# One level of Strassen's scheme for the products with w_in and w_k, and a second part ordered by a list scheduler

## The chip, the cores and the metric

One core of a Trainium2 chip runs the whole program. The metric is the device time of one execution in microseconds (us). TensorE (PE) multiplies, ScalarE (ACT) and VectorE (DVE) do the element-wise work, GpSimd (POOL) a few small copies, and SyncE (SP) issues the DMAs.

## The reference

x has shape (4, 3072, 256), so 12288 tokens of 256 channels. Cut to what matters:

```
X = rfft(x, axis=1);  Y = softshrink(complex_linear(X; w_r, w_i, b_r, b_i), 0.01);  y = irfft(Y)
h = y @ w_in                       # 256 -> 2048
g = h * tanh(softplus(h))          # "Mish"
x2 = g @ w_out                     # 2048 -> 256
xk = mu_k * x2 + (1 - mu_k) * x2_prev        # x2_prev: the token before, 0 at the start of a sequence
xr = mu_r * x2 + (1 - mu_r) * x2_prev
k = relu(xk @ w_k);  v = (k * k) @ w_v       # 256 -> 1024 -> 256
out = sigmoid(xr @ w_r2) * v
```

## The kernel before

Every product of real data is made of three TensorE products, because each operand is split into a rounded high part and a low rest: high by high, high by low, low by high. The weights come in as 64-bit words and are decoded on ACT and DVE, one piece of 256 columns (or rows) at a time, by `decode` and the `Weights` pipeline.

Part 1 is the Fourier part. It runs over 48 units, 4 sequences by 12 groups of frequencies: `emit_F`, `emit_M`, `emit_I` on TensorE, the evacuations `post_F`, `post_M`, `post_M2`, `post_I` between them, and the butterflies (`f1_ops`, `f3_ops`) as background work on DVE. In the units of the last sequence ACT and DVE also decode w_in and w_out (`win_piece`, `wout_piece`) and a rest of the other weights (`park_piece`), two steps a unit. The final butterflies of sequences 1 to 3 (six `f3_ops` jobs) run in part 2.

Part 2 takes 24 blocks of 512 tokens. For each of the 16 slices of 128 columns of w_in a step does: `emit_H` (6 matmuls of 512 columns into a PSUM bank), Mish on ACT, `dve_g` (a cast to the high part and a subtraction for the low), and `emit_acc` three steps later (6 matmuls with w_out into two accumulators). A block's accumulators are copied out (`evac`), mixed with the token before (`token_mix`) and split, all in SBUF. Between the steps of the next block stand 8 `emit_K` (6 matmuls of 512 columns each), 8 `emit_V` (12 of 256 columns each) and 2 `emit_R` (12 of 256 columns each, then a sigmoid). Where each stands is written out by hand in `PLAN`. All weights of part 2 lie in SBUF. Four PSUM banks (`psw`) rotate for the products, so a product that waits for its evacuation doesn't hold up the next. Each engine runs its instructions in the order in which they are written.

All matmuls go through the helper on line 155, all activations through line 152, tensor_tensor through 146 and scalar_tensor_tensor through 149.

Of the kernel before, what the change touches and what calls it, by code (L numbers as in the profile page):

```python
# [39 lines left out]
NPARK = 5  # L40
PARK_AT = (6, 15)

F3_PART1 = {(1, 4): [(0, 0)], (1, 8): [(0, 1)]}
F3_PART2 = {1: (1, 0), 3: (1, 1), 5: (2, 0), 8: (2, 1), 10: (3, 0), 14: (3, 1)}


SPLIT_AT = (13, 14)
EVAC_AT = 3
K_BUFS = 4
G_BUFS = 3  # L50
FILL = (900, 1500, 0)


PLAN = {
    'first': dict(K=[22, 23, 25, 27, 29, 31, 34, 36], V=[27, 27, 30, 30, 33, 33, 39, 39],
                  R=[35, 35], mix=[19, 20, 24, 25], end=40),
    'mid': dict(K=[23, 24, 25, 26, 29, 31, 35, 36], V=[28, 28, 30, 30, 34, 34, 39, 39],
                R=[33, 33], mix=[19, 20, 23, 25], end=40),
    'late': dict(K=[23, 24, 26, 28, 30, 32, 33, 36], V=[26, 28, 29, 31, 33, 35, 37, 39],
                 R=[28, 29], mix=[19, 20, 23, 25], end=40),  # L60
    'last': dict(K=[22, 23, 24, 25, 27, 28, 29, 29], V=[26, 27, 28, 29, 30, 31, 32, 33],
                 R=[25, 25], mix=[19, 20, 21, 23], end=35),
}
# [3 lines left out]
            23, 24, 25, 26, 30, 31, 28, 32, 29, 33, 34, 35, 41, 42, 36, 43, 37, 38, 44, 45, 39, 40, 46, 47]  # L67
LINES_G = [4, 5, 6, 7, 12, 13, 14, 15]
# [8 lines left out]
def dft_constants():  # L77
# [32 lines left out]
    return lay(fwd), lay(inv), sel  # L110


@with_exitstack
def tile_fft_mix_moe_channel_mix(
# [44 lines left out]
    w_dr = [dram.tile([128, 2, 512], F32, name=f"w_dr{i}") for i in range(9)]  # L159
    y_dr = [dram.tile([2, 128, 24, 128], F32, name=f"y_dr{b}") for b in range(NB)]  # L160

# [4 lines left out]
    y_p = pool(ctx, "y", 1)  # L166
    yhl_p = pool(ctx, "yhl", 2)

    mu = cst.tile([128, 2, 2], F32, name="mu")
    mu1 = cst.tile([128, 2, 2], F32, name="mu1")  # L170
# [243 lines left out]
    wt = {}  # L414

    def load_mix(h):
        raw = pools["st"].tile([128, 2, 256], F32, tag="raw", name="wraw", bufs=2)
# [18 lines left out]
    raws = []  # L436

    def raw_piece(src):
        p, tag = raws[1][raws[0] % len(raws[1])]
        raws[0] += 1  # L440
        raw = p.tile([128, 512, 2], I32, tag=tag, name="raw", bufs=2)
# [4 lines left out]
    def decode(raw, parts, scale=1.0):  # L446
        hw, lw = raw[:, :, 1], raw[:, :, 0]
        tl = {}

        def a0():  # L450
            sg = tl["sg"] = pools["st"].tile([128, 512], F32, tag="sg", name="sg")
            return [lambda: act(sg.bitcast(I32), hw.bitcast(F32), ACTF.Copy, scale=14000.0),
                    lambda: act(sg, sg.bitcast(I32), ACTF.Sign)]

        def v0():
            q = tl["q"] = pools["st"].tile([128, 512], F32, tag="q", name="q", bufs=3)
# [11 lines left out]
        def a2():  # L468
            tl["p"] = parts(tl["q"])
            return [lambda hi=hi, v=v: act(hi, v, ACTF.Copy, scale=scale) for hi, lo, v in tl["p"]]  # L470

        def v2():
            if scale == 1.0:
                return [lambda hi=hi, lo=lo, v=v: tt(lo, v, hi.bitcast(F32), SUB) for hi, lo, v in tl["p"]]
            return [lambda hi=hi, lo=lo, v=v: stt(lo, v, scale, hi.bitcast(F32), MULT, SUB)
                    for hi, lo, v in tl["p"]]
# [3 lines left out]
    def win_piece(i):  # L480
        raw = raw_piece(w_in[:, 256 * i:256 * i + 256])
        cs = slice(256 * i, 256 * i + 256)
        w = wt["in"]
        return decode(raw, lambda q: [(w[:, 0, :, cs], w[:, 1, :, cs],
                                q.rearrange("p (k f) -> p k f", k=2))])

    def wout_piece(i):
        raw = raw_piece(w_out[256 * i:256 * i + 256, :])

        def parts(q):  # L490
            ts = [mat.tile([128, 2, 256], F32R, tag="m", name="wo") for _ in range(2)]
            wt["out", 2 * i], wt["out", 2 * i + 1] = ts
            return [(ts[k][:, 0, :], ts[k][:, 1, :], q[:, 256 * k:256 * k + 256]) for k in range(2)]
        return decode(raw, parts)


    parked = ([w_k[:, 256 * i:256 * i + 256] for i in range(4)]
              + [w_v[256 * i:256 * i + 256, :] for i in range(4)] + [w_g])

    def park_piece(i):  # L500
        raw = raw_piece(parked[i])
        tl = {}

        def parts(q):
            t = tl["t"] = yhl_p.tile([128, 2, 512], F32R, tag="yl", name="wp")
            return [(t[:, 0, :], t[:, 1, :], q)]
        a0, v0, v1, a2, v2, a1 = decode(raw, parts)
        return a0, v0, v1, a2, lambda: v2() + [lambda: nc.sync.dma_start(out=w_dr[i], in_=tl["t"].bitcast(F32))], a1

    def fetch():  # L510
        for i in range(4):
            nc.sync.dma_start(out=wt["v"][:, :, 2 * i:2 * i + 2, :].bitcast(F32),
                              in_=w_dr[4 + i].rearrange("p s (c f) -> p s c f", c=2))
        nc.sync.dma_start(out=wt["g"].bitcast(F32), in_=w_dr[8].rearrange("p s (c f) -> p s c f", c=2))
        for c in range(8):
            wt["k", c] = mat.tile([128, 2, 2, 128], F32R, tag="m", name="wkt")
            src = w_dr[c // 2].rearrange("p s (h k f) -> p s h k f", h=2, k=2)
            for z in range(2):
                nc.sync.dma_start(out=wt["k", c][:, z].bitcast(F32), in_=src[:, z, :, c % 2, :])
# [27 lines left out]
    NBLK = NB * N // 512  # L547
    yt = {}

    def load_y(j):  # L550
        b, o = divmod(j, N // 512)
        t = y_p.tile([128, 2, 512], F32, tag="y", name="y")
        for h in range(2):
            nc.sync.dma_start(out=t[:, h, :], in_=y_dr[b][h, :, 4 * o:4 * o + 4, :].rearrange("p n f -> p (n f)"))
        yt[j] = t

    yhl = {}

    def split_y(j, h):
        if h == 0:  # L560
            yhl[j] = (yhl_p.tile([128, 2, 512], F32R, tag="yh", name="yh"),
                      yhl_p.tile([128, 2, 512], F32R, tag="yl", name="yl"))
        hi, lo = yhl[j][0][:, h, :], yhl[j][1][:, h, :]
        y = yt[j][:, h, :]
        l = [lambda: tt(lo, y, hi.bitcast(F32), SUB)]
        if j:
            return [lambda: act(hi, y, ACTF.Copy)], l
        return [], [lambda: V.tensor_copy(hi, y)] + l


    def part1():
        with ExitStack() as es:
# [6 lines left out]
            raws[:] = [0, [(st_p, "raw"), (st_p, "raw"), (yhl_p, "yh")]]  # L579
# [152 lines left out]
            NU = NB * NT  # L732

            pe, bg.clock = START
            x_at, y_at = bg.clock, 0.0
            for u in range(NU):
# [9 lines left out]
                if u == NU - NT - 1:  # L746
                    wt["in"] = big.tile([128, 2, 2, 2048], F32R, tag="big", name="win")
                    todo = [lambda: win_piece(0)]
# [5 lines left out]
                    wq = Weights(todo[:6] + late + todo[6:])  # L754
                    wq.load(3)
# [3 lines left out]
                elif PARK_AT[0] <= u < PARK_AT[1]:  # L759
                    dec = 1  # L760
                    if u == PARK_AT[0]:
                        wq = Weights([lambda i=i: park_piece(i) for i in range(NPARK)])
# [35 lines left out]
                if b == NB - 1 and t == 10:  # L798
                    bg.drain()
                    load_y(0)  # L800
# [3 lines left out]
            for h in range(2):  # L804
                emit(split_y(0, h)[1])
# [7 lines left out]
    def part2():  # L813
        with ExitStack() as es:
            ch_p = pool(es, "ch", 2)
            gh_p = pool(es, "gh", G_BUFS)
            x2_p = pool(es, "x2", 1)
            xk_p = pool(es, "xk", 1)

            pool(es, "gap", 1).tile([128, 16], F32, name="gap")  # L820
            xr_p = pool(es, "xr", 1)
            kk_p = pool(es, "kk", 2)
            sg_p = pool(es, "sg", 1)
            psw = pool(es, "psw", 4, space=PSUM)
            psa = pool(es, "psa", 1, space=PSUM)
            psv = pool(es, "psv", 1, space=PSUM)

            b1 = big.tile([128, 8192], F32R, tag="big", name="b1")
            wt["v"] = b1[:, 0:4096].rearrange("p (s c f) -> p s c f", s=2, c=8)
            wt["g"] = b1[:, 4096:5120].rearrange("p (s c f) -> p s c f", s=2, c=2)  # L830
            xk = [b1[:, 1024 * i:1024 * i + 1024].rearrange("p (c f) -> p c f", c=2) for i in (5, 6, 7)]
            xk = [tuple(xk[:2]), (xk[2], xk_p.tile([128, 2, 512], F32R, name="xkl1"))]
# [234 lines left out]
```

## Time and profile before

| | |
|---|---|
| median of 3 runs | 1982.35 us (1982.24 to 1982.41) |
| span of the profiled execution | 1979.9 us; its time around the span isn't listed by itself, and the median of the runs lies 2.45 us above it |
| TensorE busy, matmuls | 1958.0 us (99%), 10084 |
| DVE busy, ACT busy | 1141.4 us (58%), 929.0 us (47%) |
| part 1, part 2 on TensorE | to 327.2 us, then to 1975.2 us |
| granted TensorE clock | 1.00 in each stretch that was read |

A matmul's busy time overlaps that of the next one, so that the time from start to start, and not the duration, tells what a matmul takes. For ACT and DVE the durations of instructions that follow each other overlap by about 0.1 us.

### The profile page before, as it was taken

To read this page: it belongs to the slowest core of one execution; us is meant where nothing else is said; L and a number is where in the kernel's file an instruction comes from. 1 tells how busy PE (TensorE), PEld (TensorE's weight loads), DVE (VectorE), ACT (ScalarE), POOL (GpSimd) and SP (SyncE) were. 2 spreads that over 40 slices of the span, in tenths; PEclk is the share of its full clock that TensorE was granted. 3 is DMA by queue.
4 is the path that set the end of the run, shared out by engine and by line. 5 is a ranking of instruction groups with operands and counts; after the bars stand their busy time and mean duration, and the time that the engine had idled before them with its cause. 6 is when DMAs were issued, how large, how long until landed. Compare 5 with 4: busy or idle time off the path is not lost.

```text
span 1979.9 us, 25685 instructions
## 1 busy us (share of the span) xinstructions
PE 1958.0 (99%) x10084; PEld 1686.2 (85%) x10084; DVE 1141.4 (58%) x2183; ACT 929.0 (47%) x1525; POOL 13.2 (1%) x28
## 2 busy tenths in 40 slices
PE   6999999999999999999999999999999999999999
PEld 5888888888888888888888888888888888888888
DVE  8999976665654754465375445555544544444444
ACT  2422286344544554454445444444544544454455
POOL 0000000000000000000000000000000000000000
PEclk9999999999999999999999999999999999999999
DMA  9445276111011010101101001011000000000000
GB/s 279 150 138 170 70 245 200 39 32 65 22 33 54 22 44 11 54 22 33 54 22 54 1 22 54 5 33 38 22 1 22 22 11 12 22 23 1 22 11 22
DMA packets 104554, 106.66 MB, mean 54 GB/s; under 512 B 7017, under 2 KB 85489, under 8 KB 103409
## 3 DMA queue, kind: packets, MB, share of 16 engines
q1 hardware_dynamic: 104432, 105.02, 16.7%
q8 instruction: 79, 1.29, 0.3%
q14 instruction: 43, 0.34, 0.1%
HBM read 62.53 MB, written 42.47 MB: 53 GB/s over the span
## 4 chain that ended last, share of the span: by engine, by line
PE 97%; DMA 1%; DVE 1%; ACT 0%; issue 0%; SPq 0%; DVEq 0%; ACTq 0%
PE a L155 26%; PE hps L155 26%; PE v L155 14%; PE kps L155 13%; PE yps L155 7%; PE bps L155 4%; PE xps L155 4%; PE zps L155 3%; DMA a<-in_x_dram 1%; DMA w_dr<-wp 0%; DVE g L146 0%; ACT sg L152 0%; SPq L266 0%; DVE q L149 0%; ACT q L152 0%
## 5 line engine op out<-in xcount | busy, mean ns | idle before, releaser
L863 DVE CAST gh<-u 128x512 fp32r<-128x512 f32 x384 | 163.2, 425 | 747.5 <-PE a L155 598.2
L155 PE MATMUL a<-gh,wo 128*128 128x512 f32 x1536 | 536.3, 390 | 0.0
L155 PE MATMUL hps<-yh,win 128*128 128x512 f32 x1536 | 534.7, 389 | 0.0
L152 ACT ACTIVATE u<-hps 128x512 f32<-128x512 f32 x384 | 229.7, 598 | 525.0 <-PE hps L155 368.8
L155 PEld LDWEIGHTS hps<-yh,win 128*128 128x128 f32 x1536 | 288.3, 188 | 60.3
L155 PEld LDWEIGHTS a<-gh,wo 128*128 128x128 f32 x1536 | 288.4, 188 | 58.0
L155 PE MATMUL a<-gl,wo 128*128 128x512 f32 x768 | 299.9, 390 | 0.0
L155 PE MATMUL hps<-yl,win 128*128 128x512 f32 x768 | 298.8, 389 | 0.0
L155 PE MATMUL kps<-b,wkt 128*128 128x512 f32 x960 | 280.1, 390 | 0.0
L155 PE MATMUL v<-b,kh 128*128 128x256 f32 x1536 | 275.8, 281 | 0.0
L146 DVE TENSOR_TENSOR gl<-u,gh 128x512 fp32r<-128x512 f32 x384 | 263.6, 687 | 3.6
L155 PEld LDWEIGHTS v<-b,kh 128*128 128x128 f32 x1536 | 243.7, 190 | 7.6
L155 PE MATMUL v<-b,kl 128*128 128x256 f32 x768 | 215.8, 281 | 0.0
L155 PEld LDWEIGHTS kps<-b,wkt 128*128 128x128 f32 x960 | 179.1, 188 | 36.1
L152 ACT ACTIVATE ka<-kps 128x512 f32<-128x512 f32 x192 | 115.0, 599 | 185.5 <-PE kps L155 185.5
L155 PEld LDWEIGHTS hps<-yl,win 128*128 128x128 f32 x768 | 144.1, 188 | 29.9
L155 PEld LDWEIGHTS a<-gl,wo 128*128 128x128 f32 x768 | 144.5, 188 | 26.6
L146 DVE TENSOR_TENSOR kl<-ka,kh 128x512 fp32r<-128x512 f32 x192 | 132.5, 690 | 32.8 <-ACT ka L152 19.1
L155 PEld LDWEIGHTS v<-b,kl 128*128 128x128 f32 x768 | 144.1, 188 | 0.0
L152 ACT ACTIVATE ka<-ka 128x512 f32<-128x512 f32 x192 | 121.4, 632 | 6.3
L152 ACT ACTIVATE kh<-ka 128x512 fp32r<-128x512 f32 x192 | 121.4, 632 | 6.3
L146 DVE TENSOR_TENSOR g<-g 128x128 f32<-128x128 f32 (+3 forms) x272 | 107.5, 433 | 1.2
(80 smaller groups left out, 1926.8 us busy)
## 6 DMA issues: line engine op xcount, KB each, us to landing
b_dr<-bs SPq DMA_DIRECT2D x48, 256.0 KB, 2.2
g<-b_dr SPq DMA_DIRECT2D x8, 1536.0 KB, 6.8
y<-y_dr SPq DMA_DIRECT2D x48, 256.0 KB, 3.2
out_dram<-r SPq DMA_DIRECT2D x48, 256.0 KB, 2.2
y_dr<-g SPq DMA_DIRECT2D x80, 64.0 KB, 1.6
w_dr<-wp SPq DMA_DIRECT2D x9, 512.0 KB, 5.9
a<-in_x_dram SPq DMA_DIRECT2D x8, 512.0 KB, 6.2
y_dr<-g SPq DMA_DIRECT2D x32, 128.0 KB, 1.9
```

The source lines that it names most:

```text
L146: V.tensor_tensor(out=o, in0=a, in1=b, op=op)
L152: S.activation(out=o, in_=i, func=f, **kw)
L155: T.matmul(out=o, lhsT=l, rhs=r, start=start, stop=stop, **kw)
L863: return [lambda: V.tensor_copy(hi, u), lambda: tt(lo, u, hi.bitcast(F32), SUB)]
```

## The change

**The scheme.** The products with w_in and w_k are made in blocks of 2 by 2 by 2: the 256 channels in two halves, 1024 tokens in two halves of 512, and 256 columns of the weight as two slices of 128. Of the 8 block products the Winograd form of Strassen's scheme needs 7 (each of three matmuls). Its sums of weights are made once, at decoding (`pair_pieces`), and stored in DRAM (`h_dr`, `k_dr`); its sums of data are made once per 1024 tokens (`mix_sum`, `part_hi`, `part_lo`, in `moving`). Its sums of results are made in PSUM: ACT copies a partial result from one bank to another, later matmuls add to the copy, and DVE adds two results to SBUF (`k12`, `k22`).

**Two phases.** Phase A does all 12 superblocks of 1024 tokens through w_in and w_out, 8 groups each. The mixed tokens go to DRAM (`xk_dr`, `xr_dr`). Phase B reads them back and does w_k, w_v and the gate, 4 groups for each superblock. In phase A the sums of w_in come from DRAM group by group, four DMAs each, into a ring of two groups (`load_ring`). w_v and the gate's weight are decoded late in phase A.

**The order.** The class `Plan` takes each step with an engine, an assumed duration, a due time and the steps it needs, runs through the time of the five engines and calls the steps in the order that comes out. The hand-written `PLAN` and `FILL` go. TensorE's banks are now x, z, c, d, one buffer each, and four accumulators.

The diff, cut to its core:

```diff
+    def pair_pieces(w, dst, i, m, field, stage):          # part 1; two raw pieces, 512 KB each
+            def sums():
+                return v1() + [lambda: tt(s(1), s(4), s(0), SUB), lambda: tt(s(2), s(6), s(1), SUB),
+                               lambda: tt(s(5), s(6), s(4), SUB), lambda: tt(s(7), s(3), s(2), SUB)]
+            def highs():
+                t = f["t"] = stage()
+                return [lambda: act(t[:, 0:4, 0, :], f["s"][:, 0:4, :], ACTF.Copy),
+                        lambda: act(t[:, 4:7, 0, :], f["s"][:, 5:8, :], ACTF.Copy)]
+            def lows():
...
+                put = lambda g: nc.sync.dma_start(
+                    out=dst[2 * i + g], in_=t.rearrange("p m s f -> p (m s) f")[:, :, 128 * g:128 * g + 128].bitcast(F32))
...
+def load_ring(g, k):
+        m = 2 if k < 3 else 1
+        nc.sync.dma_start(out=ring[4 * (g % 2) + k][:, 0:2 * m, :].bitcast(F32), in_=h_dr[g % 8][:, 4 * k:4 * k + 2 * m, :])
...
-                    for i in range(8):
-                        if i < 7:
-                            todo.append(lambda i=i: win_piece(i + 1))
-                        todo.append(lambda i=i: wout_piece(i))
-                    late = [lambda i=i: park_piece(i) for i in range(NPARK, 9)]
+                    for i in range(4):
+                        todo += pair_pieces(w_in, h_dr, i, 4, lambda i=i: wfield[:, i % 2], lambda i=i: half[i % 2])
+                    todo += [lambda i=i: wout_piece(i) for i in (0, 4, 1, 5, 2, 6, 3, 7)]
...
+            def group(n, tiles, need, weights, outs):
...
+                    def go():                              # product()
+                        mm(o, h, c[:, 0, k, :], start, False, skip_group_check=True)
+                        mm(o, h, c[:, 1, k, :], False, False, skip_group_check=True)
+                        mm(o, l, c[:, 0, k, :], False, True, skip_group_check=True)
...
+                m1 = add("PE", 0.68, b, product(0, "x", True), need(0), x_free)
+                m5 = add("PE", 0.68, b + 0.02 * T, product(1, "z", True), need(1), z_free)
+                p11 = add("ACT", 0.48, b, copy("p11"), m1, c_free)
+                zs = add("ACT", 0.48, b + 0.25 * T, still, m5, zs_free)
+                m6 = add("PE", 0.68, b + 0.25 * T, product(2, "x", False), need(2), p11)
+                m2 = add("PE", 0.68, b + 0.27 * T, product(3, "p11", False), need(3), p11)
+                p12 = add("ACT", 0.48, b + 0.25 * T, copy("p12"), m6, d_free)
+                m7 = add("PE", 0.68, b + 0.5 * T, product(4, "x", False), need(4), p12)
+                m3 = add("PE", 0.68, b + 0.52 * T, product(5, "p12", False), need(5), p12)
+                p21 = add("ACT", 0.48, b + 0.5 * T, copy("p21"), m7)
+                k22 = add("DVE", 0.62, b + 0.5 * T, plus("k11", "p21"), p21, zs, last_read.get("k11"))
+                k12 = add("DVE", 0.62, b + 0.52 * T, plus("k01", "p12"), m3, zs, last_read.get("k01"))
+                m4 = add("PE", 0.68, b + 0.8 * T, product(6, "p21", False), need(6), k22)
+                x_free, z_free, d_free, zs_free = p21, zs, k12, [k12, k22]
+                first, c_free = outs(n, {(0, 0): m2, (0, 1): k12, (1, 1): k22, (1, 0): m4})
+                plan.after(p21, [first])
...
+            def f32_H(kind, key, ps, tiles, due, src, old_f, old_h):       # phase A: four results a group
+                if ps is None:                             # k12, k22: from SBUF
+                    f = add("ACT", 0.54, due, lambda: act(cur[key], cur[key], ACTF.Mish), src)
+                    return f, add("DVE", 0.34, due, lambda: V.tensor_copy(tiles()[0], cur[key]), f, old_h), None
...
+                f = add("ACT", 0.48, due, mish, src, old_f)
+                if kind == (0, 0):
+                    h = add("ACT", 0.48, due, lambda: act(tiles()[0], cur[ps], ACTF.Mish), src, old_h)
...                                                        # then for each: lo on DVE, and a unit on PE
+            def unit_H(n, kind, st):                       # 6 matmuls of 512 columns with w_out
...
+            def f32_K(kind, key, ps, tiles, due, src, old_f, old_h):       # phase B: Relu, Square, Square on ACT,
+                                                           # or max*mult on DVE and a Copy on ACT; lo on DVE
+            def unit_K(n, kind, st):                       # 12 matmuls of 256 columns with w_v
...
+            def moving(key, b0, pace, load, old, *prev):   # 4 sums on DVE, 7 high parts on ACT, 7 low parts on DVE
+            def gate(J, q, need):                          # 12 matmuls of 256 columns into bank z, then Sigmoid
```

## Rows read from the trace of the kernel before

**Rows 1.** The page's head and its first part: busy time, share, instructions.
```profile
span 1979.9 us, 25685 instructions
PE 1958.0 (99%) x10084; PEld 1686.2 (85%) x10084; DVE 1141.4 (58%) x2183; ACT 929.0 (47%) x1525; POOL 13.2 (1%) x28
```
**Rows 2.** The chain that ended last, share of the span by engine.
```profile
PE 97%; DMA 1%; DVE 1%; ACT 0%; issue 0%; SPq 0%; DVEq 0%; ACTq 0%
```
**Rows 3.** The tile hps: ns min/median/max, first and last start; groups by line, v.
```profile
L155 PE MATMUL hps<-yh,win x1536: 388/389/580, 327.2 to 1933.4; 128*128 128x512 f32 x192
...
L155 PE MATMUL v<-b,kh 128*128 128x256 f32 x1536 | 275.8, 281 | 0.0
```
**Rows 4.** The timeline of part 2, single matmuls: start, duration (us).
```profile
328.32 0.39 PE L155 MATMUL hps<-yl,win 128*128 128x512 f32 x1
...
331.05 0.39 PE L155 MATMUL hps<-yl,win 128*128 128x512 f32 x1
...
703.23 0.28 PE L155 MATMUL zps<-b,xrl 128*128 128x256 f32 x1
...
704.64 0.28 PE L155 MATMUL zps<-b,xrl 128*128 128x256 f32 x1
```
**Rows 5.** The chain that ended last, in order of time: start, length, what.
```profile
303.64 2.96 PE yps L155 x13
310.05 2.96 PE yps L155 x13
...
1970.26 4.96 PE v L155 x42
```
**Rows 6.** Stretches: busy time (x instructions), granted clock, DMA share, GB/s.
```profile
5.00:10.00 5.00, 0.00 (x0) 0.00 (x0) 2.58 (x3) 0.59 (x1) 0.00 (x0) 1.00 1.03 281
10.00:15.00 5.00, 0.00 (x0) 0.00 (x0) 3.55 (x6) 1.84 (x3) 0.00 (x0) 1.00 1.07 313
...
290.00:300.00 10.00, 9.74 (x44) 7.91 (x43) 8.63 (x16) 9.90 (x21) 0.00 (x0) 1.00 0.94 314
```
**Rows 7.** The timeline: from a matmul to ACT, from ACT to DVE.
```profile
323.73 0.39 PE L155 MATMUL yps<-bias,pick 128*128 128x512 f32 x1
...
324.15 0.60 ACT L152 ACTIVATE yb<-yps 128x512 f32<-128x512 f32 x1 [2.36 <-PE yps L155]
...
329.56 0.60 ACT L152 ACTIVATE u<-hps 128x512 f32<-128x512 f32 x1
...
330.20 0.43 DVE L863 CAST gh<-u 128x512 fp32r<-128x512 f32 x1 [4.72 <-ACT u L152]
```
**Rows 8.** Groups by line: busy us, mean ns; idle before and its releasers.
```profile
L146 DVE TENSOR_TENSOR gl<-u,gh 128x512 fp32r<-128x512 f32 x384 | 263.6, 687 | 3.6
L152 ACT ACTIVATE u<-hps 128x512 f32<-128x512 f32 x384 | 229.7, 598 | 525.0 <-PE hps L155 368.8 <-issue 116.5 <-DVE gl L146 36.1
L863 DVE CAST gh<-u 128x512 fp32r<-128x512 f32 x384 | 163.2, 425 | 747.5 <-PE a L155 598.2 <-ACT u L152 149.3
...
L152 ACT ACTIVATE ka<-ka 128x512 f32<-128x512 f32 x192 | 121.4, 632 | 6.3
L146 DVE TENSOR_TENSOR g<-g 128x128 f32<-128x128 f32 (+3 forms) x272 | 107.5, 433 | 1.2
...
L152 ACT ACT_TABLE_LOAD x49 | 62.9, 1283 | 10.3 <-DMA braw<-in_b_r_dram 9.4
...
L149 DVE SCALAR_TENSOR_TENSOR g<-g 128x512 f32<-128x512 f32 (+1 forms) x84 | 50.9, 620 | 0.0
```
**Rows 9.** Who waited for whom: us in total, times, longest.
```profile
ACT u L152 <- DVE gl L146: 36.1, 17, 3.1
```
**Rows 10.** DMA issues, KB each, us to landing; SP's timeline.
```profile
y<-y_dr SPq DMA_DIRECT2D x48, 256.0 KB, 3.2
...
11.43 0.43 SPq L419 DMA_DIRECT2D wraw<-in_w_i_dram  x1
11.90 0.43 SPq L418 DMA_DIRECT2D wraw<-in_w_r_dram  x1
```

More of the change, by code (lines that the diff above doesn't have):

```diff
@@ L1 @@
+import heapq
 from contextlib import ExitStack
@@ L110, in dft_constants, with __init__, add, after @@
     return lay(fwd), lay(inv), sel
+class Step:
+    __slots__ = ("eng", "hold", "done", "fn", "due", "need", "users", "ready", "end")
+class Plan:
+    AFTER = {"PE": 0.2, "ACT": 0.19, "DVE": 0.16, "POOL": 0.3, "SP": 0.0, "-": 0.0}
+    def __init__(self):
+        self.steps = []
+    def add(self, eng, hold, due, fn, *need, land=0.0):
+        s = Step()
+        s.eng, s.hold, s.due, s.fn = eng, hold, due, fn
+        s.done = hold + self.AFTER[eng] + land
+        s.need, s.users, s.ready, s.end = 0, [], 0.0, None
+        self.after(s, need)
+        self.steps.append(s)
+        return s
+    def after(self, s, need):
+        for d in need:
+            if isinstance(d, (list, tuple)):
+                self.after(s, d)
+            elif d is not None:
+                d.users.append(s)
+                s.need += 1
+    def run(self):
+        free = dict.fromkeys(self.AFTER, 0.0)
+        wait = {e: [] for e in self.AFTER}
+        now = {e: [] for e in self.AFTER}
+        count = 0
+        self.idle = []
+        def put(s):
+            nonlocal count
+            heapq.heappush(wait[s.eng], (s.ready, count, s))
+            count += 1
+        for s in self.steps:
+            if not s.need:
+                put(s)
+        left = len(self.steps)
+        while left:
+            best = None
+            for e in free:
+                t = free[e]
+                if not now[e]:
+                    if not wait[e]:
+                        continue
+                    t = max(t, wait[e][0][0])
+                if best is None or t < best[0]:
+                    best = (t, e)
+            t, e = best
+            while wait[e] and wait[e][0][0] <= t:
+                _, k, s = heapq.heappop(wait[e])
+                heapq.heappush(now[e], (s.due, k, s))
+            s = heapq.heappop(now[e])[2]
+            s.fn()
+            left -= 1
+            if e == "PE" and t > free[e] + 0.01:
+                self.idle.append((free[e], t - free[e], s.due))
+            free[e] = t + s.hold
+            s.end = t + s.done
+            for u in s.users:
+                u.need -= 1
+                u.ready = max(u.ready, s.end)
+                if not u.need:
+                    put(u)
+        return free
 @with_exitstack
@@ L455, in v0 @@
         def v0():
-            q = tl["q"] = pools["st"].tile([128, 512], F32, tag="q", name="q", bufs=3)
+            q = tl["q"] = place()
             qi = q.bitcast(I32)
@@ L492, in parts @@
             wt["out", 2 * i], wt["out", 2 * i + 1] = ts
[L493 to L501, printed above, removed]
+            return [(ts[k][:, 0, :], ts[k][:, 1, :], q[:, k, :]) for k in range(2)]
+        return decode(raw, flat_q, parts)
@@ new lines, in f3_job @@
+            def f3_job(b, h, t0, w, prev):
+                load, ops = f3_ops(b, h)
+                last = add("SP", 0.1, t0, load, prev, land=9.0)
+                stores = []
+                for k, (cost, fn) in enumerate(ops):
+                    due = t0 + 10 + w * k / len(ops)
+                    if cost:
+                        last = add("DVE", cost / 1000, due, fn, last)
+                    else:
+                        stores.append(add("SP", 0.1, due, fn, last, land=3.0))
+                return [last] + stores
@@ L1033, in tile_fft_mix_moe_channel_mix @@
+            plan.run()
     with tc.manual_schedule():
```

677 lines of the change are left out of this document (407 added, 270 removed).

## The prediction

> **What bounds the kernel now.** I read the page's busy times first: TensorE is busy for 99% of the span, DVE for 58%, ACT for 47% [rows 1]. Busy time alone doesn't prove a bound, since the durations of matmuls overlap, so I went to the chain that ended last: 97% of it is TensorE [rows 2]. Then I checked the rate. In the timeline 12 matmuls of 512 columns start in 331.05 - 328.32 = 2.73 us, 0.2275 us each; 12 of 256 columns in 704.64 - 703.23 = 1.41 us, 0.1175 us each [rows 4]. Part 2 has 24 x (16 x 12 + 8 x 6) = 5760 of the first kind and 24 x (8 x 12 + 2 x 12) = 2880 of the second: 1310.4 + 338.4 = 1648.8 us. On the trace it goes from 327.2 us [rows 3] to 1970.26 + 4.96 = 1975.2 us [rows 5], 1648.0 us. So part 2 is TensorE's issue rate and nothing else, and a matmul taken out there is worth its 0.2275 us as long as TensorE never waits.
>
> **What the change takes away.** A group of 1024 tokens by 256 columns had 8 block products of 3 matmuls, and has 7. There are 12 x 8 groups in phase A and 12 x 4 in phase B, 144 in all, so 144 x 3 = 432 matmuls of 512 columns go: 432 x 0.2275 = 98.3 us. The products with w_out (2304 matmuls), w_v (2304) and the gate (576) stay. A group of phase A is 21 + 24 matmuls, 10.24 us; one of phase B is 21 of 512 columns and 48 + 12 of 256, 11.83 us. With no wait at all the span would be 1979.9 - 98.3 = 1881.6 us.
>
> The Trainium skill, "TensorE: Matmul & The Clock Gate", section "Back-to-back issue gap", gives about 131 ns for a sustained matmul of 512 columns; by it the 432 would be worth 57 us and the time would be some 42 us longer than forecast. The trace of this kernel disagrees, with 227.5 ns start to start.
>
> **What it adds on ACT and DVE.** New operations have no row of their own. The nearest for an ACT copy from PSUM to PSUM are 598 ns (PSUM to SBUF) and 632 ns (SBUF to SBUF); for DVE's sums 687 ns, for its casts 425 ns [rows 8]. Per group of phase A, ACT does 4 copies and 5 Mish, about 9 x 0.6 = 5.4 us, and its share of the superblock's 7 high parts, 4 evacuations and 8 mixes, some 1.5 us: 6.9 of 10.24 us. DVE does 2 sums, 3 casts and 4 low parts (1.4 + 1.3 + 2.75 us), and 11 operations of the moving data and 8 mixes per superblock, 1.6 us: 7.1 of 10.24 us. In phase B, ACT does 4 copies, 2 x 3 for the results in PSUM, 2 for those in SBUF, a sigmoid and 11/4 high parts: 9.7 of 11.83 us. DVE does 8 operations and about 4.75 of the moving data, the gate and the end: 8.8 us. The six butterfly jobs left are (107.5 + 50.9) / 8 = 19.8 us each [rows 8]; a pair of them over some 12 groups raises DVE there to about 10.3 us by durations, about 9 if the overlap of neighbouring instructions is taken off. So neither engine is the bound, but both come near it. Sigmoid and Mish no longer alternate: nearly all of the 49 table loads of 1.28 us go. They were covered by TensorE's work, so this only gives ACT room.
>
> **Does TensorE wait within a group?** This is the main risk: its banks x, c, d have one buffer, and in each group three links run from a product through ACT (and once DVE) back to a product. From the last matmul's start to ACT is 324.15 - 323.73 = 0.42 us, that is 0.19 after its slot; ACT to DVE is 330.20 - 330.16 = 0.04 us [rows 7], which I take for ACT to PE and DVE to PE too. Links m1-p11-m6 and m6-p12-m7: 0.19 + 0.60 + 0.04 = 0.83 us. Link m7-p21-k22-m4: 0.19 + 0.60 + 0.04 + 0.69 + 0.04 = 1.56 us. The cover is a neighbouring product (0.68 us) and one unit of the group before (6 x 0.2275 = 1.37 us): 2.05 us. So the slack is 1.2, 1.2 and 0.5 us. The units are ready a group ahead: from m4 to its unit is about 0.19 + 0.60 + 0.43 + 0.69 plus two steps of 0.04, 2 us of 10.24. The third link breaks only where ACT or DVE is in the middle of another instruction with over 0.5 us to go, and then another unit can stand in, since the order was made with such durations in view. Unit cover gone altogether, the links would show 0.15 + 0.15 + 0.88 = 1.18 us a group, 170 us over 144 groups. The bounds are 0 and 170 us; the slack is positive in each link, so I take a value near the lower one, 5 us (0.035 us a group).
>
> **Part 1.** The sums add 4 short DVE operations and longer high and low parts to each pair of pieces, but fewer pieces are decoded there. What is new is traffic: a pair of w_in loads 2 x 0.52 MB and stores 2 x 0.92 MB in runs of 512 bytes, and the unit stores 0.26 MB: 3.15 MB in a unit of 6.41 us (310.05 - 303.64 [rows 5]), over about 4 units. Loads of such short runs filled the DMA engines at 281 to 313 GB/s, and before the change the stretch with 314 GB/s already shows 0.26 us of idle TensorE [rows 6]. At 313 GB/s a unit's bytes take 10.1 us, 3.7 too many; four units, 15 us; at 281 GB/s, 19 us. Behind a late raw piece stand DVE's and ACT's evacuations, and TensorE waits for those. Loads that run ahead and stores that nobody waits for take part of it, and it could take all: from 0 to 19 us, I take 6.
>
> **Edges.** The first group of phase A has no units to cover it: 0.15 + 0.15 us, and a table load of 1.28 us and two Mish ahead of p21, about 2 us in all (0 to 5). Between the phases the last superblock must be evacuated before the first w_v products, which other products cover: 1.5 us (0 to 5). At the end the last unit waits for m4, Relu, two Squares and a low part (0.19 + 0.60 + 0.63 + 0.63 + 0.69, about 2.8 us) with only a few units left: 2.5 us (0 to 5).
>
> **DMA in part 2.** The ring takes 0.92 MB a group, 90 GB/s, in four transfers of up to 256 KB that land 3.2 us after issue; an issue takes SP about 0.47 us [rows 10], 1.9 us a group. They are due 1.8 groups ahead, 18 us. Cost 0: it is hidden by those 18 us unless a store that waits for DVE stands before them on SP's queue for over 10 us.
>
> **Sum.** 1881.6 + 5 + 6 + 2 + 1.5 + 2.5 = 1898.6 us of span, and 2.45 us around it as in the runs before: 1901 us.
>
> **Rivals.**
> 1. Likeliest, 0.64: as summed, 1887 to 1915 us.
> 2. The links break in the busy stretches (44 groups with butterflies, 48 of phase B): an instruction of up to 0.69 us, or a long butterfly, is in the way on DVE or ACT in most groups. At 0.3 us for 92 groups, 28 us: about 1925 us, from 1915 to 1950. For it: 82% of ACT in phase B by durations. Against: the two other links have 1.2 us. Chance 0.19.
> 3. The transfers: part 1's traffic at its upper bound, or SP held up so that the ring is late once per superblock by some 3 us: 1930 to 1975 us. For it: the DMA share of 0.94 [rows 6]. Against: 18 us of lead. Chance 0.08.
> 4. Slower: the units come late, so that nothing covers the links. The place is ACT's queue: a Mish waiting for DVE's k12 or k22 stands before the next copy, so each link pays the other's wait. At 1.18 us a group, 1884 + 170 = 2054 us; it is slower than before from 98.3 / 144 = 0.68 us a group on. For it: ACT did wait for DVE before, 36.1 us in 17 waits [rows 9]. Against: the utilisations above, and those waits were where DVE had background work first. Chance 0.07. The Trainium skill, on the same TensorE page (table of specifications), calls the queues of ScalarE and VectorE strict first-in first-out; that is what would make one wait pay for others, and the longest of those waits, 3.1 us, agrees.
> 5. The matmuls taken out are worth less than their neighbours' 0.2275 us, each tenth less costing 9.8 us: half as much would give 1950 us. Every row read has the same rate, so 0.01. The rest, 0.01, is left out.
>
> **From the cases to the numbers.** The forecast is that of case 1, 1901 us. Its own range is 1887 to 1915. For 8 in 10 I go down to 1886, nearly the bound without a wait (1884 with what lies around the span), and up into case 2 and a part of case 3, to 1932. About 0.2% (4 us) is what a measurement can tell from no change. Faster are the cases 1, 2, 5 and nearly all of 3, 0.92; within 4 us of the time before 0.01; slower 0.07.
>
> **What would show it.** Right: 5328 matmuls of 512 columns in part 2 at 0.2275 us; each group of phase A close to 10.24 us from its first product to the next group's, of phase B 11.83; TensorE's idle time some 20 us above that of before, with the largest piece in the last quarter of part 1, released by a DMA through DVE or ACT; 3 or so table loads. Wrong: TensorE waiting in each group for DVE's k11 (the third link), which grows with the butterflies; waits for ring tiles released by DMA; or a granted clock under 1.00 in a stretch where TensorE waits often, which the trace of before never shows [rows 6].

## The result and the profile after

The changed kernel takes 1938.83 us (1933.15 to 1940.15 over 4 runs) against 1982.38 us: a ratio of 0.9775, 95% interval 0.9761 to 0.9788, so 2.2% faster. The forecast was 1901 us and the range ended at 1932: the sign was right, the time was missed by 38 us. The page and the groups by line after the change, in the form of [rows 1, 2, 8]:

```profile
span 1937.4 us, 26749 instructions
PE 1878.8 (97%) x9654; PEld 1611.2 (83%) x9654; DVE 1397.8 (72%) x2565; ACT 1210.2 (62%) x2141; POOL 7.6 (0%) x16
...
PE 87%; DVE 4%; DMA 4%; ACT 4%; issue 1%; SPq 0%; ACTq 0%; DVEq 0%
```
```profile
L207 ACT ACT_TABLE_LOAD x15 | 19.2, 1283 | 9.5 <-DMA braw<-in_b_r_dram 9.3
```

TensorE still carries the chain, but with 87% in place of 97%; DVE, DMA and ACT take 4% each. The 10084 recorded matmuls have become 9654; 432 gone would leave 9652. Table loads fell from 49 to 15, not to 3.

The last product of part 1 (tile bps) starts at 341.9 us, before the change at 327.2: 14.7 us later. (In the traces of experiments 2 to 5, which leave part 1 as it is, it starts at 340.2 to 342.9 us.) From there to the last start of v it is 1591.2 us. By the prediction's count it would be 1648.8 - 98.3 = 1550.5 us with no wait, so part 2 waits for 40.7 us. The forecast had 6 and 11 us for the two. Call excess what the time from one matmul's start to the next has over its slot of 0.2275 or 0.1175 us. The 14 excesses of part 2 that are longer than 0.4 us hold 29.3 us, and 65 from 0.05 to 0.4 us hold 11.0 us, 8.5 of them in four stretches in which the granted clock was 0.50 (1.2 GHz): 1550.5 + 29.3 + 11.0 = 1590.8, so nearly all of it is in view.

Between the pieces the pace is the one predicted. Two steady stretches, in phase A and in phase B (columns as in [rows 6], by PE, PEld, DVE, ACT and POOL):

```profile
850.00:900.00 50.00, 50.00 (x222) 41.42 (x221) 35.48 (x63) 35.85 (x64) 0.10 (x1) 1.00 0.49 153
...
1500.00:1550.00 50.00, 50.00 (x342) 46.22 (x341) 32.98 (x53) 37.55 (x68) 0.00 (x0) 1.00 0.21 68
```

222 x 0.2275 = 50.5 us in a stretch of 50, with the matmuls on its edges counted: no slot is free. From the first product of a group to the next group's it is 10.2 us in the median of phase A and 11.9 in phase B, against 10.24 and 11.83 forecast.

**Four kinds of pieces** make up the loss. First, part 1. The stretch that was [rows 6]'s last line, SP's timeline there, and the chain that ended in it:

```profile
275.00:285.00 10.00, 7.42 (x33) 5.67 (x31) 8.50 (x16) 6.70 (x11) 0.00 (x0) 1.00 1.08 339
285.00:290.00 5.00, 2.51 (x6) 2.06 (x7) 4.25 (x8) 4.29 (x7) 0.00 (x0) 0.73 1.12 360
```
```profile
282.22 4.41 SPq L583 DMA_DIRECT2D h_dr<-yc  x2
286.73 3.76 SPq L499 DMA_DIRECT2D raw<-in_moe_w_out_dram  x1
```
```profile
286.73 7.53 DMA raw<-in_moe_w_out_dram
294.26 0.02 issue
294.28 0.69 ACT sg L207
```

The DMA engines are full (1.12) and TensorE is busy for half of the time. Two stores of weight sums hold SP for 4.41 us, and the raw piece behind them takes 3.76 us to issue and lands 7.53 us after it began; ACT's decoding waits for it, and behind that the evacuations.

Second, the data of the next superblock. SP, DVE, TensorE, and the windows around the longest of these pieces:

```profile
464.72 0.32 SPq L337 DMA_DIRECT2D g<-b_dr  x1
465.13 0.94 SPq L621 DMA_DIRECT2D ysrc<-y_dr  x2
```
```profile
478.47 2.02 DVE L201 TENSOR_TENSOR ysrc<-ysrc 128x512 f32<-128x512 f32 x3 [8.57 <-DMA ysrc<-y_dr]
...
483.28 0.68 DVE L201 TENSOR_TENSOR k<-c,zs 128x512 f32<-128x512 f32 x1
```
```profile
477.98 0.39 PE L210 MATMUL a<-h,wo 128*128 128x512 f32 x1
484.02 1.65 PE L210 MATMUL c<-yc,wr 128*128 128x512 f32 x3 [5.64 <-DVE k L201]
```
```profile
480.00:485.00 5.00, 0.98 (x2) 0.83 (x3) 5.00 (x7) 1.00 (x2) 0.00 (x0) 0.69 0.01 4
485.00:490.00 5.00, 5.00 (x16) 3.93 (x15) 5.00 (x13) 2.00 (x4) 0.00 (x0) 0.63 0.21 57
490.00:495.00 5.00, 5.00 (x24) 4.12 (x23) 3.19 (x10) 2.50 (x5) 0.00 (x0) 1.00 0.27 75
```

The two loads of ysrc are issued right behind a butterfly's load of 1.5 MB. The plan takes 7 us for their landing; DVE gets the data at 478.47, 13.3 us after the issue began. DVE had come to the sums of ysrc and stood there for 8.57 us; k22, which m4 needs, is behind them on the same queue. TensorE starts nothing for 6.0 us. These 6 us begin about when the data is there (477.98 and 478.47): what TensorE then waits for is the work that has piled up on DVE ahead of k22, three sums, a low part and two butterfly operations, 4.8 us up to 483.28. There is a second price: during the idle stretch the granted clock falls (0.69 and 0.63 in the mean of two windows of 5 us), and 16 matmuls are counted in 5 us where 24 stand in the next window. In narrower windows it is 0.50 from 482 to 488 us, the level of 1.2 GHz:

```profile
486.00:488.00 2.00, 2.00 (x6) 1.54 (x5) 2.00 (x5) 0.88 (x2) 0.00 (x0) 0.50 0.24 66
```

The prediction had named this as a sign of being wrong.

Third, table loads in phase A, in ACT's timeline:

```profile
740.55 1.28 ACT L207 ACT_TABLE_LOAD   x1
741.85 0.63 ACT L207 ACTIVATE dec<-dec 128x512 f32<-128x512 int32 x1
742.48 1.28 ACT L207 ACT_TABLE_LOAD   x1
743.78 0.60 ACT L207 ACTIVATE k<-c 128x512 f32<-128x512 f32 x1
744.27 0.59 ACT L207 ACTIVATE h<-c 128x512 fp32r<-128x512 f32 x1
744.88 1.28 ACT L207 ACT_TABLE_LOAD   x1
746.17 0.63 ACT L207 ACTIVATE dec<-dec 128x512 f32<-128x512 f32 x1
746.71 0.58 ACT L207 ACTIVATE c<-x 128x512 f32<-128x512 f32 x1
...
748.21 1.28 ACT L207 ACT_TABLE_LOAD   x1
```
```profile
743.24 0.39 PE L210 MATMUL a<-h,wo 128*128 128x512 f32 x1
748.18 1.65 PE L210 MATMUL c<-yc,wr 128*128 128x512 f32 x3 [4.56 <-DVE k L201]
```

The weights decoded late (tile dec) need Sign and Abs, which stand between Mish operations: four loads in 9 us. TensorE starts nothing from 743.24 to 748.18: it waits for DVE's k (k22), and that for ACT's copy c<-x (p21) at 746.71, which stands behind three of the loads.

Fourth, SP in phase B: weight loads that the plan books at 0.1 us an issue, and ACT waiting for a buffer whose store came behind them.

```profile
1360.26 3.66 SPq L1202 DMA_DIRECT2D wk<-k_dr  x4
1364.22 0.32 SPq L1205 DMA_DIRECT2D wk<-v_dr  x1
1365.00 2.50 SPq L1143 DMA_DIRECT2D xk_dr<-tm  x4
```
```profile
1369.84 0.72 ACT L207 ACTIVATE tm<-x2s,mus 128x512 f32<-128x512 f32 x1 [4.43 <-DMA xk_dr<-tm]
```

### The profile page after: what moved, and what is told of

The parts are those of the page before. It is cut to its first block, busy times and chain, and to the rows that moved or that the text cites. A ratio compares the mean times of both kernels' runs of the same rounds, so it can differ in the third digit from the quotient of the medians.

```text
span 1937.4 us, 26749 instructions
## 1 busy us (share of the span) xinstructions
PE 1878.8 (97%) x9654; PEld 1611.2 (83%) x9654; DVE 1397.8 (72%) x2565; ACT 1210.2 (62%) x2141; POOL 7.6 (0%) x16
## 4 chain that ended last, share of the span: by engine, by line
PE 87%; DVE 4%; DMA 4%; ACT 4%; issue 1%; SPq 0%; ACTq 0%; DVEq 0%
PE a L210 25%; PE x L210 14%; PE v L210 13%; PE c L210 10%; PE yps L210 5%; PE z L210 5%; PE d L210 5%; PE zps L210 3%; PE bps L210 3%; PE xps L210 3%; DMA raw<-in_moe_w_out_dram 1%; DMA wr<-h_dr 1%; ACT L207 1%; DVE a L201 1%; ACT k L207 1%
## 5 line engine op out<-in xcount | busy, mean ns | idle before, releaser
L201 DVE TENSOR_TENSOR l<-k,h 128x512 fp32r<-128x512 f32 x576 | 385.3, 686 | 376.3 <-ACT h L207 203.6
L210 PE MATMUL a<-h,wo 128*128 128x512 f32 x1536 | 531.9, 390 | 0.0
L210 PEld LDWEIGHTS a<-h,wo 128*128 128x128 f32 x1536 | 289.5, 189 | 60.5
L210 PE MATMUL a<-l,wo 128*128 128x512 f32 x768 | 299.9, 391 | 5.8 <-DVE l L201 5.8
L210 PE MATMUL v<-wv,h 128*128 128x256 f32 x1536 | 278.2, 280 | 0.0
L210 PEld LDWEIGHTS v<-wv,h 128*128 128x128 f32 x1536 | 247.5, 190 | 13.8
L210 PE MATMUL x<-yc,wr 128*128 128x512 f32 x864 | 244.8, 392 | 3.9 <-ACT c L207 3.5
L207 ACT ACTIVATE k<-k 128x512 f32<-128x512 f32 x288 | 177.1, 632 | 69.9 <-DVE k L201 67.7
L210 PE MATMUL v<-wv,l 128*128 128x256 f32 x768 | 215.3, 280 | 0.0
L207 ACT ACTIVATE k<-c 128x512 f32<-128x512 f32 x288 | 172.1, 598 | 33.6 <-PE c L210 18.0
L210 PEld LDWEIGHTS c<-yc,wr 128*128 128x128 f32 x576 | 108.1, 189 | 38.5 <-DVE k L201 16.4
L210 PE MATMUL bps<-im,yb 128*128 128x256 f32 x384 | 93.3, 387 | 10.5 <-DVE yb L204 10.5
```

The lines of the kernel that those rows point to most:

```text
L201: V.tensor_tensor(out=o, in0=a, in1=b, op=op)
L207: S.activation(out=o, in_=i, func=f, **kw)
L210: T.matmul(out=o, lhsT=l, rhs=r, start=start, stop=stop, **kw)
```

## The experiments

Times are medians of four or five runs, but for experiments 4, 5 and 10, which ran once; before is some 1982 us in each. "Part 2" is the stretch of 1591.2 us above, and gaps are excesses over 0.4 us, small excesses those from 0.05 to 0.4.

**1. Stores of whole rows in part 1.** The staged sums are laid out so that each store has 128 runs of 7168 bytes in place of 1792 of 512.

```diff
-                    out=dst[2 * i + g], in_=t.rearrange("p m s f -> p (m s) f")[:, :, 128 * g:128 * g + 128].bitcast(F32))
+                    out=dst[2 * i + g], in_=t[:, g].rearrange("p m s f -> p (m s) f").bitcast(F32))
```

> Edit: the sums of the weights are staged in the order in which they are stored, so that each store of 0.92 MB is 128 runs of 7168 bytes and no longer 1792 runs of 512; bytes, instructions on ACT, DVE and TensorE and their elements stay. In the changed kernel TensorE's part 1 ends at 342.2 us, 14.7 us later than before, with five gaps between 267 and 307 us. Theory A (the queue is held up by the many short runs: the raw pieces behind them come late): the gaps go, part 1 ends near 330 us, the whole is 12 to 15 us shorter, about 1925 us. Rival 1 (bytes: 3.15 MB a unit are too many whatever their runs): the gaps stay, within 3 us. Rival 2 (the sums and the longer high and low parts overload DVE or ACT): the gaps stay, released by ACT or DVE and not by the raw pieces.

1930.37 us, 0.9735 (0.9719 to 0.9751). Part 1's last product starts at 334.7 in place of 341.9 us, 7.2 earlier, and part 2 stays at 1591.25. The same windows and SP's stores:

```profile
275.00:285.00 10.00, 7.81 (x34) 5.98 (x33) 9.83 (x20) 7.33 (x12) 0.00 (x0) 1.00 1.03 386
285.00:290.00 5.00, 4.35 (x20) 3.81 (x21) 4.97 (x8) 4.94 (x9) 0.00 (x0) 1.00 1.00 370
```
```profile
281.77 0.81 SPq L584 DMA_DIRECT2D h_dr<-yc  x2
282.68 0.87 SPq L499 DMA_DIRECT2D raw<-in_moe_w_out_dram  x1
```

A pair of stores holds SP for 0.81 us, not 4.41, more bytes flow, and the clock stays at 1.00. But half of the loss is still there, five gaps of 1.3 to 1.8 us with DVE at 9.83 of 10 us. So short runs are about half of part 1's loss (5.5 to 8.2 us by the traces of experiments 2 to 5), and the other half looks like DVE. Whether the raw piece was late by SP's longer issue or by what the DMA engines spent on the short runs isn't separated: both changed.

**2. No Sign and no Abs in the decoding.** Both become Copy, so the decoding of the weights leaves out the sign and the absolute value, with the same instructions otherwise.

```diff
-                a2 = add("ACT", 0.54, due + 8, lambda: act(sg(), sg().bitcast(I32), ACTF.Sign), a1)
+                a2 = add("ACT", 0.54, due + 8, lambda: act(sg(), sg().bitcast(I32), ACTF.Copy), a1)
-                a3 = add("ACT", 0.54, due + 10, lambda: act(q_(), q_(), ACTF.Abs), v2)
+                a3 = add("ACT", 0.54, due + 10, lambda: act(q_(), q_(), ACTF.Copy), v2)
```

> Edit: in the late decoding of w_v and the gate's weight ACT's Sign and Abs are left out (Copy stands in their place), so that part of the computation is not done; their time is that of Copy. Theory A (the table loads that Sign and Abs bring between Mish, 12 of 1.28 us, hold up the copies of the groups from 740 to 837 us): the 15 table loads fall to 3, the seven gaps of that stretch (9.7 us with the slower clock after the longest, 1.6 us more) go, 9 to 11 us shorter, about 1928 us. Rival (what holds up is the wait for the raw piece at the head of DVE and ACT, 3.5 and 2.5 us): only the small gaps go, 3 us at most.

1924.39 us, 0.9708 (0.9693 to 0.9722). 3 loads are left, and part 2 takes 1576.1 us, 15.1 less. TensorE's matmuls come in the same order in both kernels, so that each can be held against itself: between 738 and 841 us, where the 12 loads were, 10.5 us are won, which is what the theory said. The 12 loads are 15.4 us, so about two thirds of their time had been on the path (the slow clock behind the longest wait included). The other 4.7 us come from two places without such loads, 1.6 between 477 and 556 us and 3.0 behind the gap at 1369 us, where the clock did not fall this time. Experiment 1, whose part 2 has no edit, differs from the changed kernel by 0.5 to 1.9 us in each of the three stretches, so the figures are no surer than that. The Trainium skill, "ScalarE: Activation LUTs", section "Table sets: the hidden batching unit", says to group calls by table set and calls abs a function that every set holds; the first agrees, the second doesn't: a load stands before the Abs at 746.17 too, with only Mish since the load before it.

**3. A later landing in the plan.** One number: when the sums of the next data are expected.

```diff
-                ld = add("SP", 0.2, b0, get, *prev, land=7.0)
+                ld = add("SP", 0.2, b0, get, *prev, land=14.0)
```

> Edit: one number in the planner: the load of the next data is taken to land 14 us after its issue and no longer 7, so that its first user is placed later on DVE and ACT. Theory A (a step that waits for this load stands at the head of DVE's queue, behind it the sums that the third link needs: the load was planned alone, but shares the queues with a butterfly load of 1.5 MB): the gaps at 353 and 478 us (5.9 and 5.8 us) go and the one at 549 (0.6), with the slow clock behind them (about 4 us), 14 to 16 us shorter, about 1923 us. Rival (DVE is simply full where the butterflies run, its busy share is 1.00 there): the gaps stay or move, within 4 us.

1917.25 us, 0.9675 (0.966 to 0.9689). Part 2 takes 1568.5 us, 22.7 less, and the gaps at 353, 478, 540 and 549 us are gone. The window that had stood still:

```profile
480.00:485.00 5.00, 5.00 (x24) 4.13 (x22) 4.92 (x13) 2.41 (x4) 0.00 (x0) 1.00 0.37 109
```

DVE is nearly as busy there as before (4.92 us of 5 against 5.00) and TensorE misses nothing, so the rival, a DVE that is simply full, fell. In the stretch of these gaps, up to 640 us, part 2 wins 16.0 us, their slow clock included, about the 14 to 16 expected. The other 6.6 lie elsewhere: 3.1 among the table loads, 13 of which remain, and 3.5 about the gap at 1369 us, since the plan comes out in another order there too (the number also stands for the loads of phase B).

**4. One ACT copy more in the tightest link.** The copy p21 is made twice, and the plan isn't told.

```diff
                         act(o, cur["x"], ACTF.Copy)
+                        if key == "p21":
+                            act(o, cur["x"], ACTF.Copy)
```

> Edit: ACT makes the copy p21 twice in each group, and the planner is not told, so the third link is 0.5 us longer in all 144 groups, with 0.5 us more of ACT. Theory A (the links have slack, the loss is in a few single waits): the prediction's slack of 0.5 us takes most of it, 0 to 0.1 us a group, up to 15 us, 1938 to 1955 us. Rival (the links are what costs, spread in small pieces): 0.4 to 0.5 us a group, 58 to 72 us, about 2000 us.

1966.41 us in a single run, 27.6 us more, 0.19 us a group; part 2 takes 28.9 us more, and the small excesses grow from 11.0 us in 65 places to 31.9 in 199. That is neither 0.1 nor 0.4 us a group, and the mean hides two phases. The second copy starts 0.61 us after the first. In phase A the median goes from 10.2 to 10.57 us between groups, and the mean rises by 0.29; phase B stays at 11.9. So the third link's slack takes 0.25 to 0.3 us of the 0.61 in phase A, less than the 0.5 of the prediction, and all of it in phase B. (That the copy's time on ACT costs nothing beside the link is taken, not shown.)

**5. Product m5 made twice**, three matmuls more in each of 144 groups, and the plan told.

```diff
+                        if idx == 1:
+                            mm(o, h, c[:, 0, k, :], start, False, skip_group_check=True)
+                            mm(o, h, c[:, 1, k, :], False, False, skip_group_check=True)
+                            mm(o, l, c[:, 0, k, :], False, True, skip_group_check=True)
```

> Edit: the second product of each group (m5) is made twice, the second time over the first, so the result stays; the planner is told. 432 matmuls of 512 columns more, as many as the scheme took away. Theory A (apart from some twenty waits the groups run at TensorE's rate): 432 x 0.2275 = 98.3 us more, 2030 to 2040 us. Rival (within the groups TensorE waits for ACT and DVE, and the extra product fills such waits): under 70 us more, under 2010 us.

2018.98 us in a single run, 80.2 more, between the two theories. The trace says why: part 2 takes 1672.6 us, its gaps 19.4 and its small excesses 4.5, and 1550.5 + 98.3 + 19.4 + 4.5 = 1672.7. The 432 matmuls take their full slots, and 16.4 us of waiting went. Some of the waits now have more work to hide behind, but the plan also came out in another order, and the two aren't separated.

**6. The four sums of weights on GpSimd**, with the whole rows of 1.

```diff
-[lambda: tt(s(1), s(4), s(0), SUB), ...
+[lambda: P.tensor_tensor(out=s(1), in0=s(4), in1=s(0), op=SUB), ...
```

> Edit: whole-row stores as in the first run of this study, and the four sums of each pair of weights on GpSimd, so that DVE does 4 x 0.34 us less for each pair of pieces. The whole-row kernel still had five gaps in part 1, 7.8 us from start to start, each released by DVE's yb. Theory A (DVE is overloaded by about 1.2 us a unit in the units that decode w_in): the five gaps shrink by 4 to 6 us, about 1925 us against 1930. Rival (the raw pieces still come late, or ACT's longer high parts are the load): the gaps stay within 1.5 us, or another engine releases them; GpSimd's own time for a sum isn't known, and if it is over some 1.5 us the pieces wait for it instead.

1931.24 us, 0.974 (0.9726 to 0.9755), the same as experiment 1. Part 1 ends 1.3 us earlier, with four gaps. DVE loses four operations a pair, about 1.56 us, but some of what is left gets slower while GpSimd works, 0.41 to 0.52 us an instruction. What remains of the relief shows: from one evacuation yb to the next it is 7.54 us, in experiment 1 8.11, so 0.6 us less. DVE and GpSimd in the same stretch:

```profile
267.48 0.68 DVE L204 SCALAR_TENSOR_TENSOR yb<-yps,yb 128x512 f32<-128x512 f32 x1
...
269.32 0.95 DVE L517 TENSOR_SCALAR wsrc<-raw 128x512 int32<-128x512 int32 x1
...
273.52 0.43 DVE L517 TENSOR_SCALAR wsrc<-raw 128x512 int32<-128x512 int32 x1
273.98 1.11 DVE L204 SCALAR_TENSOR_TENSOR wsrc<-raw,wsrc 128x512 int32<-128x512 int32 x1
275.02 0.67 DVE L204 SCALAR_TENSOR_TENSOR yb<-yps,yb 128x512 f32<-128x512 f32 x1
```
```profile
268.81 1.17 POOL L577 TENSOR_TENSOR wsrc<-wsrc 128x256 f32<-128x256 f32 x1
273.68 0.85 POOL L574 TENSOR_TENSOR wsrc<-wsrc 128x256 f32<-128x256 f32 x1 [3.70 <-DVE wsrc L204]
```

**7. Three mends together**: whole rows, the later landing, and sign and absolute value on DVE, by comparison and shifts, with nothing left out.

```diff
-                a2 = add("ACT", 0.54, due + 8, lambda: act(sg(), sg().bitcast(I32), ACTF.Sign), a1)
+                a2 = add("DVE", 0.34, due + 6, lambda: V.tensor_scalar(out=sg(), in0=words(1).bitcast(F32),
+                    scalar1=0.0, scalar2=0.5, op0=ALU.is_ge, op1=ALU.subtract), ld)
```

> Edit: whole-row stores, the load taken to land after 14 us, and in the late decoding the sign and the absolute value by DVE's comparison and shifts in place of ACT's Sign and Abs (nothing is left out). Theory A (separate causes, each with its own waits): the gains add up: 8 us from the stores, 21 from the load, 14 from the tables less what the load's run already had of it: 1896 to 1902 us. Rival (one cause behind the others, DVE being full): under two thirds of that, over 1908 us.

1902.74 us, 0.9598 (0.9582 to 0.9614), part 2 1562.2 us. The three single gains are 8.5, 14.4 and 21.6 us, together 44.5; the mend brings 36.1. Taken by stretches the causes do add up: 16.4 us of waiting go before 640 us (experiment 3 alone 16.0), 11.0 among the table loads (experiment 2 alone 10.5), and part 1 ends 7.5 us earlier (experiment 1 alone 7.2). What was counted twice is what 2 and 3 had each won elsewhere; at 1369 us 6.4 of 7.8 us of waiting are still there.

**8. SP as slow in the plan as on the chip**: 0.45 us an issue, and later landings of the stores and loads of phase B.

```diff
+        if eng == "SP":
+            hold *= 4.5
...
-                ld = add("SP", 0.1, due, begin, prev, land=5.0)
+                ld = add("SP", 0.1, due, begin, prev, land=9.0)
```

> Edit: as the run before it, and the planner is told what issuing costs SP (0.45 us a DMA and not 0.1), and later landings for the butterfly loads (13 us), the stores of the mixed tokens (4.5), the raw pieces of w_v (9) and the gate's data (10). Theory A (the gap of 4.3 us at 1369 us stands behind a token mix on ACT that waits for a store, which waited on SP behind some 13 issues of weight loads): that gap goes with the slow clock behind it, 4 to 6 us shorter than the run before it, about 1894 us. Rival (the last superblock's chain of evacuation, mix and store is too long whatever the order on SP): the gap stays.

1897.77 us, 0.9571 (0.9557 to 0.9586): 5.0 us less, and 4.3% faster than before. The gap at 1369 us, 4.15 us in the changed kernel and 3.20 in experiment 7, is 1.20, and about it 3.2 us of waiting go; the other 2 go before. Part 2 takes 1556.9 us, 6.4 above its bound, and the clock falls nowhere in it. This is the best version. The stretch with all butterflies, and what is left of part 1's loss, in its waits between 245 and 342 us:

```profile
352.00:717.00 365.00, 363.85 (x1602) 300.23 (x1601) 329.51 (x666) 229.94 (x406) 1.58 (x4) 1.00 0.55 174
```

```profile
PE bps L213 <- DVE yb L207: 6.0, 5, 1.4
```

**9. Pairs of w_in and pieces of w_out decoded in turn**, on top of 8, and the first tokens' sums a unit later.

```diff
                         todo += pair_pieces(w_in, h_dr, i, 4, lambda i=i: wfield[:, i % 2], lambda i=i: half[i % 2])
-                    todo += [lambda i=i: wout_piece(i) for i in (0, 4, 1, 5, 2, 6, 3, 7)]
+                        todo.append(outs.pop(0))
+                    todo += outs
```

> Like the kernel before it in this series (whole-row stores, late landings and SP issues told to the planner, Sign and Abs on DVE: 1897.8 us), and in part 1 the pairs of w_in and the pieces of w_out are decoded alternately instead of all pairs first. Theory (what is left of part 1's loss is DVE's load, 8.1 us in each unit in which a pair's steps fall against 6.4 us of TensorE): with a w_out piece between, DVE has about 6.6 us to do in a unit on average, so the five gaps of 1.4 to 1.8 us in part 1 (7.2 us together) shrink to 1 to 3 us and the time is 1892 to 1894 us. Rival (the gaps come from what else stands on DVE in those units, or the sums of the first tokens, started later, hold up part 2's start): the gaps move but their sum stays, or a gap of some us appears at the start of part 2: 1896 to 1902 us.

1899.1 us, 0.9582 (0.9569 to 0.9595), so the rival: the gaps moved, and their sum, from start to start, is 6.9 us against 7.9. Part 1's last product starts at 334.8 us in both. Spreading the work didn't help, which left the question whether DVE's load is the cause at all.

**10. The four sums of weights made twice**, on top of 8.

```diff
-                return v1() + [lambda: tt(s(1), s(4), s(0), SUB), ...
+                return v1() + 2 * [lambda: tt(s(1), s(4), s(0), SUB)] + ...
```

> The version with all three mends (1897.8 us; last product of part 1 at 334.8 us, five gaps of 1.2 to 1.8 us there), with each of the four sums of a pair of w_in pieces made twice on DVE: 4 x 0.39 = 1.56 us more of DVE for each of four pairs, nothing else. Theory (in the units of the pairs DVE's own work, 8.1 us against 6.4 us of TensorE, sets part 1): all of it shows, 4 to 6.2 us; the last product of part 1 starts at 339 to 341 us. Rival (DVE has room and the gaps come from late raw pieces or from the order of single instructions): less than 2 us of it shows; 335 to 337 us.

1910.26 us in a single run; part 1's last product starts at 344.8 us, 10 us later than in 8, more than either theory had. DVE's timeline, first of 8, then of 10:

```profile
268.62 0.68 DVE L207 SCALAR_TENSOR_TENSOR yb<-yps,yb 128x512 f32<-128x512 f32 x1
...
274.19 1.56 DVE L204 TENSOR_TENSOR wsrc<-wsrc 128x256 f32<-128x256 f32 x4
...
276.73 0.68 DVE L207 SCALAR_TENSOR_TENSOR yb<-yps,yb 128x512 f32<-128x512 f32 x1
```
```profile
265.68 0.68 DVE L207 SCALAR_TENSOR_TENSOR yb<-yps,yb 128x512 f32<-128x512 f32 x1
...
271.26 3.40 DVE L204 TENSOR_TENSOR wsrc<-wsrc 128x256 f32<-128x256 f32 x8
...
275.64 0.68 DVE L207 SCALAR_TENSOR_TENSOR yb<-yps,yb 128x512 f32<-128x512 f32 x1
```

From one evacuation yb to the next it is 8.11 us in 8 and 9.96 in 10: 1.85 more, and the sums take 3.40 - 1.56 = 1.84 more. All of it shows, as the 0.6 us less did in experiment 6. So in the units with a pair DVE sets the pace, not a DMA. The expectation was low because the pairs of w_k, decoded in the first sequence, show it too: 3.3 of the 10 us lie before 113 us.

## Why the prediction was wrong

By its own steps:

- **"Cost 0: it is hidden by those 18 us" failed, and it is the largest miss.** The ring was indeed never late. But the step looked only at the ring and at SP's lead. The loads that came late were those of ysrc, behind 1.5 MB; DVE's and ACT's steps on them were placed by assumed landings and issues that the chip doesn't keep, and on an in-order engine a step that waits for data stops the links behind it. By the trace of experiment 3 the late ysrc cost 16.0 us where its waits were; experiment 8 puts another 5.3 (1562.2 to 1556.9) on SP's time and other landings. Rival 3 had the size, at a chance of 0.08, and its first half, part 1's traffic near its upper bound, was not far off, but in part 2 it named the ring. The lower clock, which the prediction named as a sign and put at nothing in the sum, is inside these numbers: 8.5 of the 40.7 us of waiting, behind the four longest waits.
- **"Nearly all of the 49 table loads … go" failed.** 12 of the 15 left belong to the late decoding, whose operations on ACT weren't listed at all. They cost 10.5 us of part 2 (experiment 2, between 738 and 841 us). The prediction's own reason for the loads being free before, TensorE's work as cover, no longer held once a group's links ran through ACT. This and the first point lie in different stretches, and in experiment 7 they add up.
- **Part 1 was mis-sized**: 6 us were taken, 14.7 measured, inside the bounds of 0 to 19. The place and the sign (the last quarter, released by a DMA through ACT and DVE) were right for half: about 7 us from runs of 512 bytes (experiment 1). The other half is DVE's own work, 8.1 us in a unit of 6.4 (experiments 6 and 10), which the text mentioned as "4 short DVE operations" and didn't sum.
- **98.3 us was right**: against the changed kernel, without the excesses of either, experiment 5 puts the same 432 matmuls at 97.8 us (1648.7 - 1550.9). Rival 5 fell.
- **The links were right in what they cost**: the steady stretches run at the full rate, so 5 us was rather too much. The slack of the third link was put too high in phase A, 0.25 to 0.3 in place of 0.5 us (experiment 4). Rival 2 gave 1925 us, nearer to the result than the forecast, but for a reason that the steady stretch of phase B and, in experiment 8, the stretch of the butterflies (363.85 of 365 us busy) exclude; rival 4 fell as a whole, though its mechanism, one wait on a queue paying for others, is what made the late loads so dear.
- **The edges were small, as said**: with the mends, part 2 is 6.4 us above its bound, start, phase change and end included; 11 had been taken with the links.

The sum of the forecast, 1901 us, is about what the scheme is worth where loads, table switches and SP's time are booked as the chip has them: experiment 8 takes 1897.8 us. Two misses offset each other in that agreement: part 1 still loses 7.6 us in place of 6, part 2 6.4 in place of 11. What stays open is how to take the last 7 us out of part 1: neither GpSimd nor another order did, and after the reordering w_out's raw pieces were on the chain too.

## What to carry to other kernels

Before a transfer is costed at nothing, follow what waits for it: on an in-order engine, one step whose load lands 6 us later than planned holds up everything behind it, however much lead the other transfers have. In a plan made from assumed durations, compare the assumed landing and issue times with the trace first; changing numbers in the plan alone brought 21.6 and 5.0 us here. List what an edit puts on each engine over the whole program, late decoding and its table switches too, and sum it by unit, since an average over a phase hides units that are over full.

## What the runs showed that was not expected

- A store of 0.92 MB held SP's issue for 2.2 us in runs of 512 bytes and for 0.4 us in runs of 7168 bytes, and the load issued behind the short runs took 3.76 us to issue in place of 0.87 (experiment 1).
- Some of DVE's instructions slow beside GpSimd's additions of 0.7 to 1.2 us: a TENSOR_SCALAR takes 0.95 in place of 0.43 us and a SCALAR_TENSOR_TENSOR of two tiles in SBUF 1.11 in place of 0.70, while the evacuations yb and xl, which read PSUM, keep their 0.68 us (experiment 6). The Trainium skill, "SBUF — State Buffer", section "SBUF: two separate sides", describes a port pair that DVE and GpSimd share and that one of them holds for a whole instruction, where DVE's instruction is in a two-port mode or has two inputs in SBUF; these rows agree, with delays of 0.52 and 0.41 us inside one addition. In which mode the TENSOR_SCALAR ran no row here shows.
- During the 6.0 us in which TensorE started nothing the granted clock fell to 1.2 GHz, and it came back some time after the matmuls did, so that such a wait costs more than its length: 16 matmuls instead of 24 in a window of 5 us behind it. The length of one wait doesn't tell it: the clock fell at one of 3.57 us in experiment 5 (at 352 us) and stayed at 1.00 at one of 3.88 us in experiment 2 (at 1355 us).
